# Two first-layer feature tiles in one product scheme, for thirteen more pairs of tiles: a tuned attention and feed-forward kernel on one Trainium2 core

## The chip, the core and the metric

The kernel runs on one core of one Trainium2 chip. A core has engines that each work through a list of instructions of their own, in the order of that list: TensorE does matrix products (PE in the profile, its weight loads PEld), VectorE element-wise work (DVE), ScalarE activations and copies (ACT), GpSimd (POOL) and SyncE (SP) here mostly start transfers. They meet through semaphores: an instruction that needs another engine's result waits, and everything behind it in its list waits with it. Products land in PSUM, which is divided into banks; all else is kept in SBUF. The metric is device microseconds of one execution, lower is better.

## The reference

All data is float32. The first half is a recurrence over 768 steps for 4 batches and 8 heads of 48 channels, and the second half a feed-forward layer over the 3072 tokens of 384 channels that it gives:

```python
for t in range(S):                                   # attention, per batch and head
    cur = np.einsum('bhd,bhe->bhde', u[None] * kt, vt)
    y[:, :, t] = np.einsum('bhd,bhde->bhe', rt, state + cur)
    state = wt[:, :, :, None] * state + np.einsum('bhd,bhe->bhde', kt, vt)

x = attn_out.transpose(0, 2, 1, 3).reshape(B * S, H * D)      # 3072 x 384
h = x @ w_in                                         # 384 -> 2048
g = h - np.tanh(h)
return (g @ w_out).astype(np.float32)                # 2048 -> 384
```

## The kernel before

The tokens are cut into 8 blocks of 384 (a batch and one of its halves each, numbered 0 to 7). The outer loop runs over the blocks, the inner over the 16 feature tiles f = 0 to 15 of 128 features. While a block goes through its feed-forward layer, the attention of the next block is threaded between its tiles, so that TensorE always has products to do. The order on every engine is the order in which the Python code issues the instructions. No scheduler changes it, and it was arranged by hand.

**A plain feature tile.** `first` (L887) multiplies three 128x128 pieces of `w_in` by the three 128x384 pieces of the block's tokens `xT`, which are summed in the PSUM bank `hp`. The profile counts two passes for each float32 product, so a tile has 6 passes of 384 columns. `slight` then has ScalarE read `hp` twice (two tanh, L975 and L976) and square the first (L979, with a second record for its accumulator), and VectorE multiplies the two (L894) to g. The first layer of the next plain tile needs `hp` free again, and so ScalarE's two reads of it done.

**The second layer in fewer products.** For two tiles, that is a pair q = f // 2, g @ w_out takes 15 products of 128x128 instead of 18 (`Fewer`). They work on sums of pieces of g, which VectorE makes (`form_g`, L998, two such sums of 128x128 in one instruction), and on sums of pieces of `w_out`, kept in `forms`. Of the five instructions with sums of g for a pair one stands at its first tile (`formed`), one at its second, and three (`held_back`, then `forming`) behind the next pair's first tile. Where that pair is joined, two of these three are put off once more, to its second tile (`carried`). The products of a pair come in two parts of six, one with the next pair's first tile and one with its second. The last three of the 15 ("others", numbers 12 to 14) are put off: those of pairs 0 to 3 come together at f = 9, twelve products into a bank of their own, which ScalarE then scales out to `o` (`self.half`, L1091).

**A joined pair.** `Twos` does the first layer of two feature tiles in one scheme: on the first two of the three contraction pieces and on two halves of the tokens (HB = 192 columns) it takes 7 products for what plainly takes 8; the third piece takes 4. So a joined pair has 11 products of 128x192 (L949, 22 passes of 192 columns) where two plain tiles have 6 of 128x384 (12 passes of 384). It needs five sums of pieces of `w_in` for the pair (`weight_forms`) and four sums of token pieces for the block (`token_forms`). The products land in both banks of a double scratch named `att_...` instead of `hp`. From there one ScalarE copy (L950) and four VectorE sums (L959) give h of both tiles in SBUF, and only then `slight` runs, on h in SBUF. A VectorE list around a joined pair reads: rest of the earlier work, the first of the four sums, the sum `formed` of the pair before, the other three sums. Then come sums of products (L1114), attention work, and what was carried.

**Which pairs are joined.** `JOINED` names them by block: pair 1 in blocks 3, 4 and 5, pairs 1 and 7 in block 6, and pairs 0 to 6 in block 7, 12 in all. Pair q covers the tiles f = 2q and 2q + 1. The sums of weights of pair 1 are made anew at f = 0 of each of the blocks 3 to 6 into the left-over end of a tile for v; the results lie in a borrowed attention tile, `ks`.

Around the places that the change touches, a stage of the profile is two tiles and what is threaded between. Pairs are written by block and number below, "pair 4 of block 3" for the tiles f = 8 and 9 of block 3.

## Time and profile before

| what | value | where it stands |
|---|---|---|
| median of 3 runs | 539.9 us (539.46 to 540.0) | times |
| time of the profiled execution | 539.97 us | times |
| its span on the core | 538.2 us | page, first line |
| TensorE clock granted | 0.998 of full | times |
| PE busy | 529.1 us, 98% of the span | page, part 1 |
| DVE busy | 442.8 us, 82% | page, part 1 |
| ACT busy | 307.1 us, 57% | page, part 1 |

The profiled execution took 1.8 us more than its span, and 0.1 us more than the median. The span runs from the first to the last record on the core. PE is busy in every one of the page's 40 slices at 90% or more except the first and the last. Since matmuls are pipelined, a record may begin while the one before ends, so durations of single passes add up to more than their stretch; what a pass costs in a row is the distance from its start to the next one's start. The same holds on DVE and ACT, where one instruction starts a little before the recorded end of the last.

### The profile page before, as it was taken

What the parts mean: (1) busy time and instruction counts of PE and PEld (TensorE: products, weight loads), DVE (VectorE), ACT (ScalarE), POOL (GpSimd) and SP (SyncE); (2) the same over time, 40 slices, a digit from 0 to 9 for tenths busy, and PEclk for the clock granted to TensorE, in tenths of its full rate; (3) what the DMA queues carried; (4) which work ended last, traced back from release to release, by engine and by line L of the source; (5) the groups of instructions that cost most, each with busy time, mean ns of one, the idle gap of its engine ahead of it and who ended that gap; (6) DMA issues with size and microseconds to landing.
All of it is one profiled execution on the core that took longest, in us unless ns stands there. A gap on an engine that the chain in (4) does not pass through costs nothing.

```text
span 538.2 us, 14868 instructions
## 1 busy us (share of the span) xinstructions
PE 529.1 (98%) x5820; PEld 419.5 (78%) x5820; DVE 442.8 (82%) x914; ACT 307.1 (57%) x707; POOL 9.2 (2%) x57
## 2 busy tenths in 40 slices
PE   7999999999999999999999999999999999999996
PEld 5756665678777777877878787787878877999994
DVE  7989997698879878887887969879689798867874
ACT  4899974665546564456446564375643654435450
POOL 1100000000000000000000000000000000000001
PEclk9999999999999999999999999999999999999999
DMA  7798732352311631163121642136232410100011
GB/s 277 242 393 337 246 124 71 109 128 67 118 38 60 163 118 57 47 146 120 63 57 45 150 118 66 51 79 174 62 98 58 98 55 16 43 1 2 10 35 48
DMA packets 53047, 56.34 MB, mean 105 GB/s; under 512 B 21488, under 2 KB 50928, under 8 KB 52976
## 3 DMA queue, kind: packets, MB, share of 16 engines
q1 hardware_dynamic: 52592, 55.18, 34.1%
q8 instruction: 49, 0.80, 0.6%
q14 instruction: 22, 0.18, 0.1%
q10 hardware_dynamic: 288, 0.10, 0.1%
q0 software_dynamic: 96, 0.07, 0.1%
HBM read 44.73 MB, written 4.72 MB: 92 GB/s over the span
## 4 chain that ended last, share of the span: by engine, by line
PE 96%; DVE 1%; DMA 0%; PEld 0%; issue 0%; ACT 0%; PEldq 0%; DVEq 0%; SPq 0%
PE hp L887 36%; PE acc L1079 27%; PE att L949 8%; PE att L1079 6%; PE acc L1030 6%; PE att L773 4%; PE att L496 2%; PE att L577 2%; PE acc L1057 1%; PE att L887 1%; PE acc L887 1%; PE hp L1079 0%; DMA states<-in_wT 0%; PE att L519 0%; DVE scores L504 0%
## 5 line engine op out<-in xcount | busy, mean ns | idle before, releaser
L887 PE MATMUL hp<-xT,w_sb 128*128 128x384 f32 x594 | 208.8, 488 | 0.0
L887 PEld LDWEIGHTS hp<-xT,w_sb 128*128 128x128 f32 x594 | 106.2, 190 | 56.6 <-ACT qa L976 0.3
L1079 PE MATMUL acc<-forms,g 128*128 128x128 f32 x972 | 136.0, 276 | 0.0
L975 ACT ACTIVATE h<-hp 128x384 f32<-128x384 f32 x99 | 48.9, 494 | 145.7 <-PE hp L887 145.7
L1079 PEld LDWEIGHTS acc<-forms,g 128*128 128x128 f32 x972 | 124.4, 192 | 7.7
L998 DVE TENSOR_TENSOR g<-g 128x256 f32<-128x256 f32 x270 | 106.5, 420 | 7.2 <-PE acc L1079 2.0
L894 DVE SCALAR_TENSOR_TENSOR g<-h,qa 128x384 f32<-128x384 f32 x112 | 62.1, 554 | 56.4 <-ACT h L979 55.4
L979 ACT ACTIVATE h<-h 128x384 f32<-128x384 f32 x113 | 59.1, 523 | 0.0
L1079 PE MATMUL acc<-w_sb,g 128*128 128x128 f32 x324 | 54.1, 276 | 0.0
L1079 PEld LDWEIGHTS acc<-w_sb,g 128*128 128x128 f32 x324 | 47.0, 192 | 7.6
L976 ACT ACTIVATE qa<-hp 128x384 f32<-128x384 f32 x99 | 48.5, 490 | 0.0
L1114 DVE TENSOR_TENSOR sums<-sums 128x256 f32<-128x256 f32 x84 | 33.1, 411 | 1.3 <-ACT sums L1091 0.9
L1030 PE MATMUL acc<-w_sb,sums 128*128 128x384 f32 x96 | 33.7, 487 | 0.0
L1079 PE MATMUL att<-w_sb,g 128*128 128x128 f32 x200 | 33.4, 275 | 0.0
L266 ACT ACTIVATE up<-raw 128x768 f16<-128x768 f32 (+1 forms) x32 | 32.8, 1095 | 0.0
L1079 PEld LDWEIGHTS att<-w_sb,g 128*128 128x128 f32 x200 | 29.0, 192 | 4.2
L1030 PEld LDWEIGHTS acc<-w_sb,sums 128*128 128x128 f32 x96 | 18.1, 190 | 12.3
L431 DVE TENSOR_TENSOR_SCAN post<-w,seed 128x780 f32<-128x780 f32 x14 | 24.9, 1777 | 0.9 <-DMA w<-in_wT 0.9
L419 DVE TENSOR_TENSOR_SCAN pre<-w,start 128x780 f32<-128x780 f32 x14 | 25.0, 1783 | 0.8
L949 PE MATMUL att<-xT,w_sb 128*128 128x192 f32 x120 | 25.4, 326 | 0.0
L979 ACT ACTIVATION_READ_ACCUMULATOR h<-h 128x1 f32 x113 | 22.7, 201 | 0.0
L949 PEld LDWEIGHTS att<-xT,w_sb 128*128 128x128 f32 x120 | 19.9, 190 | 0.0
(181 smaller groups left out, 654.2 us busy)
## 6 DMA issues: line engine op xcount, KB each, us to landing
raw<-in_weights SPq DMA_DIRECT2D x16, 768.0 KB, 7.6
w<-in_wT SPq DMA_DIRECT2D x7, 780.0 KB, 4.4
k<-in_kT SPq DMA_DIRECT2D x7, 768.0 KB, 5.2
r<-in_rT SPq DMA_DIRECT2D x7, 768.0 KB, 4.4
v_sb<-in_v SPq DMA_DIRECT2D x8, 576.0 KB, 4.9
k<-in_tokens SPq DMA_DIRECT2D x7, 576.0 KB, 4.0
r<-in_tokens SPq DMA_DIRECT2D x7, 576.0 KB, 5.3
out_y<-sums SPq DMA_DIRECT2D x18, 128.0 KB, 1.9
```

The costliest lines, as they stand in the source:

```text
L266: return lambda: nc.scalar.activation(out=to, in_=of, func=AF.Copy, scale=scale, bias=bias)
L419: return nc.vector.tensor_tensor_scan(out=self.tile("pre")[:, cols], data0=self.tile("w")[:, cols], data1=start[:, 0:n * NCH * LP], initia ...
L887: nc.tensor.matmul(hp, lhsT=w_in_sb[:, f, kc, :], rhs=xT[kc], start=(kc == KC - 1), stop=(kc == 0))
L894: return lambda: nc.vector.scalar_tensor_tensor(out=out, in0=in0, scalar=scalar, in1=in1, op0=op0, op1=ALU.mult)
L949: nc.tensor.matmul(to, lhsT=lhs, rhs=rhs, start=n == 0, stop=n + 1 == len(of))
L975: made = nc.scalar.activation(out=t, in_=h, func=AF.Tanh, scale=INNER / UPSCALE)
L976: nc.scalar.activation(out=by, in_=h, func=AF.Tanh, scale=OUTER / UPSCALE)
L979: nc.scalar.activation(out=t, in_=t, func=AF.Square, accum_out=top[:, n:n + 1])
L998: return lambda: nc.vector.tensor_tensor(out=G[:, to:to + 2], in0=two(G, g_at(q, a0), g_at(q, a1)), in1=two(G, g_at(q, b0), g_at(q, b1)), ...
L1030: nc.tensor.matmul(acc, lhsT=g[:, j * P:(j + 1) * P], rhs=w_out_sb[:, f, :], start=(f == self.first), stop=(f == NF - 1))
L1079: nc.tensor.matmul(to, lhsT=G[:, g_at(q, a), :], rhs=rhs, start=start, stop=stop, skip_group_check=True)
L1114: ops.append(lambda op=op, at=at: nc.vector.tensor_tensor(out=at[0], in0=at[1], in1=at[2], op=OPS[op]))
```

## The change

Thirteen more pairs are joined: pairs 3, 4 and 7 in the blocks 3, 4 and 5, pairs 3 and 4 in block 6 (pair 7 was joined there), and pairs 4 and 7 in block 2. In the blocks 2 to 6 all joined pairs now go through one object, `beside`.

- **Sums of weights** are made once and kept in a new SBUF tile, `kept`: those of pairs 3 and 4 in block 1 at f = 8 (five instructions, 128x256 each), of pair 7 in block 2 at f = 6 and of pair 1 in block 2 at f = 10 (five of 128x128 each). The five instructions at f = 0 of each of the blocks 3 to 6 go.
- **Sums of tokens** of a block lie in a new tile `turned`; they are made at f = 1, and now in block 2 too. Block 6 no longer makes its own at f = 13 for pair 7.
- **Results** h lie in a new tile `joint`, seven rows of 192 in place of eight.
- **The "others" of pairs 0 to 3**, at f = 9, go to the bank `hp` in every block with joined pairs after block 1, where they had a half of the double scratch.
- To make room, the scratch for POOL's dynamic transfers is set to 2048 bytes. A tag of a tile in a path that is taken only for other data changes from "s" to "h".

The order on ScalarE, in block 3 from the last tile of pair 3 on, before. Here `h<-hp` is the first tanh of a plain tile, `o<-att_123` the scaling out of the twelve others, and `ks<-...` copies of the next block's attention:

```order
L979 ACTIVATE h,top<-h 128x384
L554 COPY ks<-ks 128x2x2x128
L975 ACTIVATE h<-hp 128x384
L976 ACTIVATE qa<-hp 128x384
L979 ACTIVATE h,top<-h 128x384
L554 COPY ks<-ks 128x2x2x128
L975 ACTIVATE h<-hp 128x384
L976 ACTIVATE qa<-hp 128x384
L979 ACTIVATE h,top<-h 128x384
L1091 ACTIVATE o<-att_123 128x384
L554 COPY ks<-post 128x2x2x128 x3
L975 ACTIVATE h<-hp 128x384
```

and after the change:

```order
L957 COPY joint<-att_125 128x192
L982 ACTIVATE h<-joint 128x384
L983 ACTIVATE qa<-joint 128x384
L986 ACTIVATE h,top<-h 128x384
L559 COPY ks<-ks 128x2x2x128
L982 ACTIVATE h<-joint 128x384
L983 ACTIVATE qa<-joint 128x384
L986 ACTIVATE h,top<-h 128x384
L1098 ACTIVATE o<-hp 128x384
L559 COPY ks<-post 128x2x2x128 x3
L982 ACTIVATE h<-hp 128x384
```

Both tiles of pair 4 now read `joint`, which VectorE's sums fill, the scaling out stands behind the second of them as before, and its source is `hp`, the bank that the next tile's first layer (f = 10) writes.

The order on VectorE, in block 3 from the first tile of pair 3 (f = 6) to the second of pair 4 (f = 9), before. `k<-k,r` and `diagonal<-k` are two wide steps of the next block's attention:

```order
L894 SCALAR_TENSOR_TENSOR g<-h,qa 128x384
L1114 TENSOR_TENSOR sums<-sums 128x2x128
L998 TENSOR_TENSOR g<-g 128x256
L1114 TENSOR_TENSOR sums<-sums 128x2x128
L388 TENSOR_TENSOR k<-k,r 128x1152
L894 SCALAR_TENSOR_TENSOR g<-h,qa 128x384
L998 TENSOR_TENSOR g<-g 128x256 x4
L392 TENSOR_REDUCE diagonal<-k 128x3x4x2
L894 SCALAR_TENSOR_TENSOR g<-h,qa 128x384
L1114 TENSOR_TENSOR sums<-sums 128x2x128
L998 TENSOR_TENSOR g<-g 128x256
L1114 TENSOR_TENSOR sums<-sums 128x2x128
```

and after, from the first of pair 3's four sums on:

```order
L966 TENSOR_TENSOR joint<-joint,att_125 128x2x192
L1005 TENSOR_TENSOR g<-g 128x256
L966 TENSOR_TENSOR joint<-joint,att_126 128x384
L966 TENSOR_TENSOR joint<-joint,att_126 128x192
L966 TENSOR_TENSOR joint<-joint,att_126 128x384
L1121 TENSOR_TENSOR sums<-sums 128x2x128 x2
L393 TENSOR_TENSOR k<-k,r 128x1152
L1005 TENSOR_TENSOR g<-g 128x256
L899 SCALAR_TENSOR_TENSOR g<-h,qa 128x384
L1005 TENSOR_TENSOR g<-g 128x256
L397 TENSOR_REDUCE diagonal<-k 128x3x4x2
L899 SCALAR_TENSOR_TENSOR g<-h,qa 128x384
```

and then:

```order
L1005 TENSOR_TENSOR g<-g 128x256 x2
L966 TENSOR_TENSOR joint<-joint,att_125 128x2x192
L1005 TENSOR_TENSOR g<-g 128x256
L966 TENSOR_TENSOR joint<-joint,att_126 128x384
L966 TENSOR_TENSOR joint<-joint,att_126 128x192
L966 TENSOR_TENSOR joint<-joint,att_126 128x384
```

Eight sums of h came in. The sums of g of pair 2 that were carried, and the second tile's product of pair 3, now stand behind `k<-k,r` and `diagonal<-k`, and pair 4's sums of h behind all of these.

The order on TensorE, in block 3 from the end of the others to the first layer of f = 10, before:

```order
L1079 MATMUL att_123<-w_sb,g 128x128
L1079 MATMUL acc_600<-w_sb,g 128x128 x2
L1079 MATMUL acc_600<-forms,g 128x128 x2
L1079 MATMUL acc_599<-forms,g 128x128 x2
L887 MATMUL hp<-xT_1915,w_sb 128x384
```

and after:

```order
L1086 MATMUL hp<-w_sb,g 128x128
L1086 MATMUL acc_603<-w_sb,g 128x128 x2
L1086 MATMUL acc_603<-forms,g 128x128 x2
L1086 MATMUL acc_602<-forms,g 128x128 x2
L892 MATMUL hp<-xT_1923,w_sb 128x384
```

The list is the same but for the bank: the others now fill the `hp` that the last row needs empty, with six products of pair 3 between them.

The diff, cut to its core:

```diff
-JOINED = {3: (1,), 4: (1,), 5: (1,), 6: (1, NF // 2 - 1), 7: TWOS}
+BESIDE = (1, 3, 4, 7)
+JOINED = {2: (4, 7), 3: BESIDE, 4: BESIDE, 5: BESIDE, 6: BESIDE, 7: TWOS}
+FORMED = {(1, 8): (3, 4), (2, 6): (7, 7), (2, 10): (1, 1)}
...
+    kept = const.tile([P, 5 * len(BESIDE) * P], F32, name="kept", tag="kept")
+    turned = const.tile([P, 2 * NB], F32, name="turned", tag="turned")
+    joint = const.tile([P, 7 * HB], F32, name="joint", tag="joint")
...
-            nc.scalar.copy(out=h[:, 7], in_=e0[:, 1, 0:HB])
+            nc.scalar.copy(out=h[:, 3], in_=e0[:, 1, 0:HB])
...
-                by = beside if near else twos
+                by = beside if later else twos
...
-            if later and i in JOINED and f < 2:
-                if not f:
-                    beside, v_left, late_left = (Twos(1, 1), spare_tile("v_sb", NCP * DM), spare_tile("late", NB))
-                    for x in range(5):
-                        beside.form(x, v_left, x * P)
-                    beside.results(spare_tile("ks", NPAIR * NCP * P, work))
-                    spare += beside.weight_forms(0, 2, 1, 4, 3)
-                else:
-                    spare += beside.token_forms(here, beside.halves((v_left, 5 * P), (late_left, 0)))
+            if (i, f) in FORMED:
+                spare += beside.weight_forms(0, 2, 1, 4, 3, of=FORMED[i, f])
+            if later and i in JOINED and f == 1:
+                spare += beside.token_forms(here, beside.halves((turned, 0), (turned, NB)))
...
-                    spare = (twos.token_forms(here, twos.halves((post_left, left), (ks_left, left))) +
-                             twos.weight_forms(2, 3, 4) + spare)
+                    spare = twos.weight_forms(2, 3, 4) + spare
...
-                fewer.others(ps_a, range(4))
+                fewer.others(ps_a, range(4), hp if joined else None)
...
-    nc = bacc.Bacc("TRN2", target_bir_lowering=False, num_devices=1)
+    nc = bacc.Bacc("TRN2", target_bir_lowering=False, num_devices=1, dynamic_dma_scratch_size=2048)
```

More of the change, by code (lines that the diff above doesn't have):

```diff
@@ L823, in totals @@
             nxt = dense.tile([P, NB], F32, name="tot", bufs=3 if m < 8 else 2,
-                             tag={1: "h", 2: "s", 4: "qa"}.get(m, "o"))
+                             tag={1: "h", 2: "h", 4: "qa"}.get(m, "o"))
             nxt = nxt[:, 0:n * NB // (2 * m)]
@@ L900, with __init__ @@
     class Twos:
-        def __init__(self, base, n):
-            self.base, self.n = base, n
+        def __init__(self, pairs):
+            self.pairs = pairs
             self.forms, self.to = [None] * 5, []
         def form(self, x, t, at=0):
-            self.forms[x] = t[:, at:at + self.n * P].rearrange("p (j c) -> p j c", c=P)
+            n = len(self.pairs)
+            self.forms[x] = t[:, at:at + n * P].rearrange("p (j c) -> p j c", c=P)
         def halves(self, *tiles):
@@ L914, in results, with weight_forms @@
         def results(self, *tiles):
-            self.to = [t[:, 0:8 * HB].rearrange("p (n t) -> p n t", t=HB) for t in tiles]
-        def weight_forms(self, *which):
-            at = w_in_sb[:, 2 * self.base:2 * (self.base + self.n)]
-            at = at.rearrange("p (j two) k c -> p j two k c", two=2)
+            self.to = [t[:, 0:7 * HB].rearrange("p (n t) -> p n t", t=HB) for t in tiles]
+        def weight_forms(self, *which, of=None):
+            of = of or (self.pairs[0], self.pairs[-1])
+            at = w_in_sb[:, 2 * of[0]:2 * of[1] + 2].rearrange("p (j two) k c -> p j two k c", two=2)
             (a11, a12, a13), (a21, a22, a23) = ([at[:, :, i, k] for k in range(KC)] for i in range(2))
-            s1, s2, s3, s4, s5 = self.forms
+            x0, x1 = (self.pairs.index(j) for j in of)
+            s1, s2, s3, s4, s5 = (t if t is None else t[:, x0:x1 + 1] for t in self.forms)
             every = (("add", s1, a21, a22), ("sub", s2, s1, a11), ("sub", s3, a11, a21), ("sub", s4, a12, s2),
@@ L940, in begin @@
             (a11, a12, a13), (_, a22, a23) = ([w_in_sb[:, 2 * j + i, k] for k in range(KC)] for i in range(2))
-            s1, s2, s3, s4, s5 = (t[:, j - self.base] for t in self.forms)
+            s1, s2, s3, s4, s5 = (t[:, self.pairs.index(j)] for t in self.forms)
             t1, t2, t3, t4 = self.turned
@@ L959, in begin @@
             return [lambda of=of: nc.vector.tensor_tensor(out=of[0], in0=of[1], in1=of[2], op=ALU.add)
-                    for of in ((h[:, 0:5:4], twice(h[:, 7]), both(e0[:, 0, 0:NB])),
+                    for of in ((h[:, 0:5:4], twice(h[:, 3]), both(e0[:, 0, 0:NB])),
                                (h[:, 5:7], twice(h[:, 4]), both(e1[:, 0, 0:NB])),
@@ L1003, in any_h @@
         nc.scalar.activation(out=h, in_=of, func=AF.Copy, scale=1.0 / UPSCALE)
-        s, qa = (dense.tile([P, NB], F32, name=name, tag=name) for name in ("s", "qa"))
+        s, qa = (dense.tile([P, NB], F32, name=name, tag=name) for name in ("h", "qa"))
         th, qb, big = (inp.tile([P, 2 * HALF], F32, name=name, tag=tag)[:, 0:NB]
@@ L1304 @@
     acc += [ps_d.tile([P, BANK], F32, name=f"acc{j}", tag=f"acc{j}") for j in range(1, NB // P)]
+    beside = Twos(BESIDE)
+    for x in range(5):
+        beside.form(x, kept, x * len(BESIDE) * P)
+    beside.results(joint)
     rest, formed, extra, behind, due, summed = [], [], [], [], [], []
@@ L1375 @@
                 spare += [lambda n=n: form_w(n, 4 if f < 12 else 6, 2) for n in formed_w.get(f, ())]
-            if later and i in JOINED and f < 2:
-                if not f:
-                    beside, v_left, late_left = (Twos(1, 1), spare_tile("v_sb", NCP * DM), spare_tile("late", NB))
-                    for x in range(5):
-                        beside.form(x, v_left, x * P)
-                    beside.results(spare_tile("ks", NPAIR * NCP * P, work))
-                    spare += beside.weight_forms(0, 2, 1, 4, 3)
-                else:
-                    spare += beside.token_forms(here, beside.halves((v_left, 5 * P), (late_left, 0)))
+            if (i, f) in FORMED:
+                spare += beside.weight_forms(0, 2, 1, 4, 3, of=FORMED[i, f])
+            if later and i in JOINED and f == 1:
+                spare += beside.token_forms(here, beside.halves((turned, 0), (turned, NB)))
             if i == blocks_n - 2:
                 if f == 10:
-                    twos = Twos(0, NF // 2)
-                    left = twos.n * P
-                    k_left, r_left, post_left = (spare_tile(name) for name in ("k", "r", "post"))
-                    for x, t in enumerate((k_left, r_left, post_left)):
+                    twos = Twos(range(NF // 2))
+                    left = len(twos.pairs) * P
+                    k_left, r_left = (spare_tile(name) for name in ("k", "r"))
+                    for x, t in enumerate((k_left, r_left, spare_tile("post"))):
                         twos.form(x, t)
@@ L1393 @@
                 elif f == 13:
-                    ks_left = spare_tile("ks", NPAIR * NCP * P, work)
-                    twos.form(3, ks_left)
+                    twos.form(3, spare_tile("ks", NPAIR * NCP * P, work))
                     twos.form(4, spare_tile("v_sb", NCP * DM))
-                    spare = (twos.token_forms(here, twos.halves((post_left, left), (ks_left, left))) +
-                             twos.weight_forms(2, 3, 4) + spare)
+                    spare = twos.weight_forms(2, 3, 4) + spare
                     twos.results(*(spare_tile(name) for name in ("pre", "w")))
```

## The prediction

> **What bounds the kernel now.** I read the page's first part and its chain, then PE's waits, then the stages around joined and plain pairs in windows. The chain gives one row by engine, and PE's waits are five rows of which the first is the longest:

> ```profile
> span 538.2 us, 14868 instructions
> PE 529.1 (98%) x5820; PEld 419.5 (78%) x5820; DVE 442.8 (82%) x914; ACT 307.1 (57%) x707; POOL 9.2 (2%) x57
> PE 96%; DVE 1%; DMA 0%; PEld 0%; issue 0%; ACT 0%; PEldq 0%; DVEq 0%; SPq 0%
> PE att L314 <- POOL ident masks.py:199: 2.1, 1, 2.1
> ```

> PE is the chain: 96% of it, busy for 98% of the span. So a pass taken from PE is worth its length, as long as nobody else then comes last. The windows by engine show how near DVE is to that (a row is the stretch, its length, then busy time and count of PE, PEld, DVE, ACT and POOL; the last three numbers are granted clock, DMA share and GB/s). In order they are pair 1 of block 3 (joined), a joined pair of block 7, pair 3 of block 3 (plain), its pair 4 with the twelve others (plain), and f = 0 and 1 of block 4:

> ```profile
> 224.00:230.31 6.31, 6.31 (x48) 6.31 (x47) 4.43 (x8) 4.70 (x8) 0.00 (x0) 1.00 0.28 91
> 462.98:469.23 6.25, 6.25 (x48) 6.25 (x47) 4.43 (x11) 2.05 (x8) 0.00 (x0) 1.00 0.07 16
> 238.62:245.17 6.55, 6.55 (x39) 4.96 (x38) 6.45 (x13) 3.40 (x10) 0.00 (x0) 1.00 0.51 134
> 245.17:254.40 9.23, 9.23 (x63) 7.64 (x62) 7.91 (x16) 5.43 (x15) 0.00 (x0) 1.00 0.50 149
> 278.42:283.71 5.29, 5.29 (x39) 4.50 (x37) 4.77 (x12) 1.61 (x6) 0.00 (x0) 1.00 0.08 25
> ```

> PE has no gap in any of them. In the plain pair 3 DVE is busy for 6.45 of 6.55 us: that is where this change puts eight more sums of h. The same for DVE alone, tile 9 and the tile after it:

> ```profile
> 248.44:254.40 5.96, 4.64 (x11) 1.00 0.34 97
> 254.40:259.09 4.69, 1.15 (x4) 1.00 0.15 52
> ```

> In tile 9 DVE has 5.96 - 4.64 = 1.32 us of room, and 4.69 - 1.15 = 3.54 in tile 10. What is late catches up there.

> **What PE gains.** The eleven products of a joined pair in the chain, the first second-layer products behind them, and the weight loads' group on the page (busy, mean ns of one, idle before):

> ```profile
> 224.16 3.58 PE att L949 x22
> 227.57 1.05 PE L1079 MATMUL acc<-forms,g 128*128 128x128 f32 x8
> L949 PEld LDWEIGHTS att<-xT,w_sb 128*128 128x128 f32 x120 | 19.9, 190 | 0.0
> ```

> From 224.00 to 227.57 the 22 passes take 3.57 us, .162 each. The rest of a pair, products of the second layer, is the same in a joined and a plain pair. So a pair gains 6.55 - 6.25 = .30 to 6.55 - 6.31 = .24 by the windows; I take .295, which the block 7 row supports, where less is threaded in. Thirteen pairs give 3.84 us. If all else were hidden, that would be 539.97 - 3.84 = 536.1.

> [...]

> **What DVE and ACT pay in blocks 3 to 6.** Let S be PE's start of pair 3 (238.62 in block 3). These rows give DVE's prices; a price is the distance from a start to the next start. First the sums of h of a joined pair (the first, the sum of g after it, the other three, the next; the same three cut after the second), then a product, sums of products, k times r, a product, the diagonal's reduce, and a sum of g that must wait for its product:

> ```profile
> 225.85 0.56 DVE L959 TENSOR_TENSOR ks<-ks,att 128x384 f32<-128x384 f32 x1
> 226.32 0.42 DVE L998 TENSOR_TENSOR g<-g 128x256 f32<-128x256 f32 x1
> 227.78 1.41 DVE L959 TENSOR_TENSOR ks<-ks,att 128x384 f32<-128x384 f32 x3 [1.03 <-PE att L949]
> 229.10 0.42 DVE L998 TENSOR_TENSOR g<-g 128x256 f32<-128x256 f32 x1
> 227.78 0.94 DVE L959 TENSOR_TENSOR ks<-ks,att 128x384 f32<-128x384 f32 x2 [1.03 <-PE att L949]
> 240.10 0.56 DVE L894 SCALAR_TENSOR_TENSOR g<-h,qa 128x384 f32<-128x384 f32 x1
> 240.57 0.42 DVE L1114 TENSOR_TENSOR sums<-sums 128x256 f32<-128x256 f32 x1
> 240.91 0.42 DVE L998 TENSOR_TENSOR g<-g 128x256 f32<-128x256 f32 x1
> 241.58 1.36 DVE L388 TENSOR_TENSOR k<-k,r 128x1152 f32<-128x1152 f32 x1
> 242.85 0.56 DVE L894 SCALAR_TENSOR_TENSOR g<-h,qa 128x384 f32<-128x384 f32 x1
> 244.86 1.35 DVE L392 TENSOR_REDUCE diagonal<-k 128x24 f32<-128x1152 f32 x1
> 246.12 0.55 DVE L894 SCALAR_TENSOR_TENSOR g<-h,qa 128x384 f32<-128x384 f32 x1
> 252.31 0.54 DVE L894 SCALAR_TENSOR_TENSOR g<-h,qa 128x384 f32<-128x384 f32 x1
> 252.88 0.43 DVE L998 TENSOR_TENSOR g<-g 128x256 f32<-128x256 f32 x1
> ```

> So: first sum of h .47, the three 1.32, two of them .94; a sum of g or of products .34, to its end .42; k times r 1.27; reduce 1.26; product .47, or .57 where a sum of g needs it. In pair 1 the three begin 3.78 after PE's start, when the last product has landed, and DVE idles 1.03 before. In pair 3 likewise they begin at S + 3.78, since DVE is free of f = 5 by then. Then down the list of the order after: the three to 5.10; two sums of products, the second reading the first, .79 to 5.89 (estimate: .42 and .34, and a little for the wait); k times r to 7.16; sum of g to 7.50; product and sum of g .91 to 8.41; reduce to 9.67; product of pair 3's second tile to 10.14. Behind it stand two carried sums of g, the second reading the first: 10.14 to 10.56, and 10.67 to 11.09. Then pair 4: first sum at 11.01, .47 to 11.48; sum of g to 11.82; and two of the three, after which tile 8's h is whole, .94 to S + 12.76.

> PE meanwhile starts pair 4 at S + 6.26 and reaches its products 3.57 later, at 9.83; a product is two passes, .22 (8 passes in 1.05 above, .11 apart). The third reads the first carried sum and could start at 10.27: it waits till 10.61, .34. The fifth, then at 11.05, reads the second: .09. So .43 us in each of the blocks 3 to 6. It is nothing if DVE runs .43 ahead of my sum, and .85 if it runs .4 behind; I take the sum.

> Next ACT, whose rows are the first tanh of two joined tiles that follow each other, the scaling out of the others, and three copies behind it:

> ```profile
> 230.08 0.53 ACT L975 ACTIVATE h<-ks 128x384 f32<-128x384 f32 x1
> 231.42 0.52 ACT L975 ACTIVATE h<-ks 128x384 f32<-128x384 f32 x1
> 253.26 0.49 ACT L1091 ACTIVATE o<-att 128x384 f32<-128x384 f32 x1 [1.30 <-PE att L1079]
> 253.64 2.00 ACT L554 COPY ks<-post 128x512 uint16<-128x512 uint16 x3
> ```

> A tile costs 1.34 us. Tile 8's starts when h is whole, at 12.80, ends 14.14; a copy .62 (an estimate, 2.00 for three, less the overlap) to 14.76; tile 9's to 16.10; then the scaling out, .49, to S + 16.59, and PE sees `hp` free at 16.64. Before, that scaling out (253.26, S + 14.64) read a bank that nobody waited for; now f = 10's first layer does. Without a wait PE would be there at S + 15.78 (254.40) less .59 for two pairs, plus .43: 15.62. So it waits 1.02. Behind that first layer stand all of PE's later products, so nothing hides it. From f = 6 to f = 10 a block goes from 15.78 to 16.64: +.87. The bounds: -.59, if pair 4's sums come 1.5 us earlier, so that nobody waits; +1.3, if DVE runs .4 behind my sum, since that delays PE's second layer and the scaling out alike. DVE then has the 3.54 us of tile 10 to be on time again, and pair 7 starts clean.

> **Pair 7 (blocks 2 to 5), and the rest.** With S' PE's start of f = 14, these rows are the reciprocal, the scan, the product and the next step of block 3's end:

> ```profile
> 277.43 0.22 DVE L418 RECIPROCAL start<-whole 128x12 f32<-128x12 f32 x1
> 277.69 1.78 DVE L419 TENSOR_TENSOR_SCAN pre<-w,start 128x780 f32<-128x780 f32 x1
> 279.39 0.53 DVE L894 SCALAR_TENSOR_TENSOR g<-h,qa 128x384 f32<-128x384 f32 x1
> 279.84 0.95 DVE L445 TENSOR_TENSOR post<-k,post 128x768 f32<-128x768 f32 x1
> ```

> The sums of h end at S' + 5.10; four sums of products, one narrow, 1.45 (estimate, .42 each where the next reads it) to 6.55; sum of g to 6.89; product and sum .91 to 7.80; reciprocal .26, scan 1.70, product .45 to 10.21; two carried sums end at 10.63 and, as a product's sum stands between, at 11.31. PE starts f = 0 of the next block at S' + 6.26, and its six products end that stage's 5.29 us: they begin 3.96 in, the third at 10.66 (.02 late), the fifth at 11.12 (.24 late). So .26 is paid and .295 gained, -.03 a block, bounds -.295 (sums on time) and +.3. Block 6 had pair 7 joined already: 0.

> Block 2 gets pair 4 without pair 3. Its k times r and its stage before:

> ```profile
> 180.53 1.36 DVE L388 TENSOR_TENSOR k<-k,r 128x1152 f32<-128x1152 f32 x1
> 181.44:190.67 9.23, 9.23 (x63) 7.64 (x61) 8.54 (x17) 5.44 (x15) 0.00 (x0) 1.00 0.29 88
> ```

> k times r ends .4 us into the pair, when its products have not landed yet, so DVE is not behind: tile 8's h is whole 3.78 + .94 = 4.72 in, two tiles and a copy end 3.3 later, at 8.0, and the scaling out at 8.5; PE needs `hp` at 9.23 - .295 = 8.94. Hidden, -.295, with its pair 7 (-.03) -.33 in all. The new sums of weights are fifteen instructions of .34 (128x256) or less, 1.75 us in block 1 and 1.0 twice in block 2. I take 0, since they stand where DVE has room in the block shown (3.54 us in f = 10); if none of it were hidden they would cost 3.75, if a tenth .4. Five such go from f = 0 of each of the blocks 3 to 6, where DVE was busy for 4.77 of 5.29 us: 0 too, for DVE is not late there before, with -.3 at best where pair 7's sums would be late. The others in `hp` in block 7: `hp` lies idle there until f = 14, 0.

> Sum: -.33 + 3 x (.87 - .03) + .87 = +3.06, on 539.97 (.1 over the median): 543.0.

> **The rivals.** All hidden, 536.1: for it speak the 57% of ACT and the 82% of DVE; against it the 6.45 of 6.55 above. It decides at S + 15.1 for the end of the scaling out, 1.5 us before my sum. It is the one on the other side. Half hidden: the carried sums come in time, the bank's wait is left at about .65: a block then loses .65 - .59 = .06 in pairs 3 and 4 and gains .295 in pair 7, so .06 x 4 - 3 x .295 - .59 = -1.24, 538.7. The backlog lasts: DVE still late in f = 11 to 13, another .5 to 1 us in each of four blocks, 545 to 547; the 3.54 us idle speak against. The transfers: POOL's three, whose scratch gets small, stand in the first block (the second row is a transfer of the same chip with its time to landing):

> ```profile
> L793 POOL DMA_DIRECT2D xT<-late x3: 487/487/619, 17.6 to 18.6; - x3
> out_y<-sums SPq DMA_DIRECT2D x18, 128.0 KB, 1.9
> ```

> At two further landings of 1.9 us they would add up to 3.8 on the forecast, 546.8; they are issued within 1.0 us in the first 19 us, and I see no need of them then. Weight loads pace narrow passes: 22 x .190 = 4.18 us instead of 3.57 to 3.89, +.29 x 13 = +3.8, 543.7 alone; the 3.58 of the chain rules it out.

> **How the numbers follow.** My forecast .68 (its own range 541 to 545, from the bounds of the three waits taken halfway), all hidden .10, half hidden .12, lasting backlog .06, transfers .03, weight loads .01. Leaving out the first rival, and the top of the backlog, gives 538.5 to 545.2. 0.2% or 1.1 us is what a measurement of this kernel can tell from no change: faster is the first rival and most of the half hidden one, .17; same .06; slower .77.

> **What the profile after would show.** PE idle before the first layer of f = 10, waiting for ACT's `o<-hp`, about 1.0 us four times; PE waiting for a sum of g in four blocks, .34 and .09 a time, and at f = 0; joined pairs of 6.25 to 6.31 us where nothing waits; PE's busy time about 3.8 lower, near 525.3; DVE's about 23 higher by the thirteen pairs' sums. Wrong if the scaling out ends by S + 15.1, if DVE catches up inside pair 3, or if a joined pair takes longer beside attention work than in block 7.

## The result: 1.4% slower, by more than the waits that were forecast

The changed kernel took 547.21 us in the median of four runs (545.76 to 548.68), the kernel before 539.94 in the same session. The ratio is 1.0137 with an interval of 1.0101 to 1.0172. The forecast was 543.0 us, its range 538.5 to 545.2. The direction was right; the time lies above the range. Two of the four runs took 545.76 and 545.99, two, the profiled one among them, 548.43 and 548.68.

The profiled execution took 548.68 us, 8.7 us more than the one before (span 547.0 for 538.2). The page's first lines and chain, and PE's waits (in total, times, longest):

```profile
span 547.0 us, 14920 instructions
PE 531.2 (97%) x5950; PEld 439.2 (80%) x5950; DVE 464.8 (85%) x961; ACT 310.4 (57%) x720; POOL 9.2 (2%) x57
PE 86%; DVE 7%; ACT 3%; issue 1%; DMA 1%; PEld 0%; SPq 0%; PEldq 0%; DVEq 0%
```

```profile
PE hp L892 <- ACT o L1098: 2.9, 4, 0.7
PE att L778 <- issue: 2.5, 2, 1.9
PE att L316 <- POOL ident masks.py:199: 2.1, 1, 2.1
PE att L501 <- issue: 1.5, 1, 1.5
PE att L501 <- ACT k L461: 1.0, 1, 1.0
PE acc L1086 <- DVE g L1005: 0.8, 4, 0.2
```

The chain is no longer PE's alone. Two rows were forecast, `hp` waiting for the scaling out (four times) and `acc` waiting for sums of g (four times). Two more were not: "issue", time in which PE waited for nothing that the profile shows. The stages by engine (stretch, length, busy time of PE, PEld, DVE, ACT, POOL, clock, DMA share, GB/s): pair 4 of block 2; pairs 3 and 4 of block 3; f = 0 of block 4; then f = 12 and f = 13 of block 6, and the end of that f = 13.

```profile
181.72:190.65 8.93, 8.93 (x72) 8.93 (x71) 6.86 (x15) 5.39 (x15) 0.00 (x0) 1.00 0.31 92
239.51:245.77 6.26, 6.26 (x49) 6.26 (x47) 5.25 (x11) 2.06 (x8) 0.00 (x0) 1.00 0.88 255
245.77:256.14 10.37, 9.44 (x73) 9.05 (x71) 10.13 (x21) 6.56 (x18) 0.00 (x0) 1.00 0.26 80
279.98:285.64 5.66, 5.66 (x38) 4.63 (x37) 5.59 (x12) 2.65 (x8) 0.00 (x0) 1.00 0.35 104
458.36:466.71 8.35, 6.41 (x212) 5.20 (x211) 8.00 (x20) 1.61 (x6) 0.18 (x2) 1.00 0.24 73
466.71:471.74 5.03, 5.03 (x20) 3.88 (x19) 2.18 (x3) 3.00 (x8) 0.00 (x0) 0.66 0.11 28
468.00:471.74 3.74, 3.74 (x16) 3.02 (x14) 0.89 (x2) 1.82 (x6) 0.00 (x0) 0.54 0.14 33
```

The first four are the forecast's stages: pair 4 of block 2 gains (9.23 before), pair 3 gains (6.55), pair 4 of block 3 loses (9.23), f = 0 loses (5.29). The fifth and sixth are new. Before, they were

```profile
453.40:459.60 6.20, 6.20 (x212) 5.21 (x211) 5.73 (x17) 1.61 (x6) 0.18 (x2) 1.00 0.32 97
459.60:462.98 3.38, 3.38 (x26) 2.58 (x19) 3.35 (x5) 2.77 (x7) 0.00 (x0) 1.00 0.10 21
```

so block 6 loses 2.15 us in f = 12, where PE stands still, and 1.65 in f = 13, where PE is busy throughout but at a granted clock of 0.54 over its last 3.74 us (the trace's clock records have 0.50 for 3.41 us from 468.10 on). The rows of PE where it stood still, in blocks 2 and 6:

```profile
204.17 1.55 PE L778 MATMUL att<-scores,v_sb 64*48 64x64 f32 x93 [0.53 <-issue]
...
466.57 0.21 PE L778 MATMUL att<-scores,v_sb 64*48 64x64 f32 x1 [1.94 <-issue]
```

Where the 8.7 us are, by the distance between the starts of the blocks' first matmuls: block 2 +0.24, blocks 3, 4 and 5 +1.03 to +1.05 each, block 6 +5.13, block 7 -0.05; before block 1 +0.27. Of these, 0.82 (block 2, f = 12) and 3.80 (block 6, f = 12 and 13) are the new part, 4.6 us. The rest of blocks 2 to 7 is 3.8 us, which the prediction put at 3.06.

### The profile page after: what moved, and what is told of

Its sections match the earlier page's. It is cut to its first block, busy times and chain, and to the rows that moved or that the text cites. A ratio compares the mean times of both kernels' runs of the same rounds, so it can differ in the third digit from the quotient of the medians.

```text
span 547.0 us, 14920 instructions
## 1 busy us (share of the span) xinstructions
PE 531.2 (97%) x5950; PEld 439.2 (80%) x5950; DVE 464.8 (85%) x961; ACT 310.4 (57%) x720; POOL 9.2 (2%) x57
## 3 DMA queue, kind: packets, MB, share of 16 engines
HBM read 44.73 MB, written 4.72 MB: 90 GB/s over the span
## 4 chain that ended last, share of the span: by engine, by line
PE 86%; DVE 7%; ACT 3%; issue 1%; DMA 1%; PEld 0%; SPq 0%; PEldq 0%; DVEq 0%
PE hp L892 26%; PE acc L1086 23%; PE att L956 14%; PE acc L1037 6%; PE att L778 4%; PE att L1086 3%; PE att L501 2%; DVE joint L966 2%; PE att L582 2%; PE hp L1086 1%; PE acc L1064 1%; DVE g L1005 1%; PE att L892 1%; DMA r<-in_rT 1%; DVE k L393 1%
## 5 line engine op out<-in xcount | busy, mean ns | idle before, releaser
L892 PE MATMUL hp<-xT,w_sb 128*128 128x384 f32 x438 | 155.2, 491 | 2.9 <-ACT o L1098 2.9
L1086 PE MATMUL acc<-forms,g 128*128 128x128 f32 x972 | 138.3, 278 | 0.8 <-DVE g L1005 0.8
L892 PEld LDWEIGHTS hp<-xT,w_sb 128*128 128x128 f32 x438 | 78.7, 191 | 48.6 <-ACT o L1098 3.7
L982 ACT ACTIVATE h<-hp 128x384 f32<-128x384 f32 x73 | 36.0, 493 | 102.0 <-PE hp L892 101.9
L1086 PE MATMUL acc<-w_sb,g 128*128 128x128 f32 x324 | 55.3, 280 | 0.0
L956 PE MATMUL att<-xT,w_sb 128*128 128x192 f32 x250 | 53.0, 326 | 0.0
L966 DVE TENSOR_TENSOR joint<-joint,att 128x384 f32<-128x384 f32 (+1 forms) x72 | 34.6, 501 | 17.6 <-PE att L956 10.0
L982 ACT ACTIVATE h<-joint 128x384 f32<-128x384 f32 x36 | 18.7, 519 | 44.6 <-DVE joint L966 44.6
L956 PEld LDWEIGHTS att<-xT,w_sb 128*128 128x128 f32 x250 | 41.5, 190 | 0.0
L983 ACT ACTIVATE qa<-hp 128x384 f32<-128x384 f32 x73 | 35.7, 489 | 0.0
## 6 DMA issues: line engine op xcount, KB each, us to landing
out_y<-sums SPq DMA_DIRECT2D x18, 128.0 KB, 1.9
```

Source lines behind the costliest of these rows:

```text
L892: nc.tensor.matmul(hp, lhsT=w_in_sb[:, f, kc, :], rhs=xT[kc], start=(kc == KC - 1), stop=(kc == 0))
L956: nc.tensor.matmul(to, lhsT=lhs, rhs=rhs, start=n == 0, stop=n + 1 == len(of))
L966: return [lambda of=of: nc.vector.tensor_tensor(out=of[0], in0=of[1], in1=of[2], op=ALU.add) for of in ((h[:, 0:5:4], twice(h[:, 3]), both ...
L982: made = nc.scalar.activation(out=t, in_=h, func=AF.Tanh, scale=INNER / UPSCALE)
L983: nc.scalar.activation(out=by, in_=h, func=AF.Tanh, scale=OUTER / UPSCALE)
L1086: nc.tensor.matmul(to, lhsT=G[:, g_at(q, a), :], rhs=rhs, start=start, stop=stop, skip_group_check=True)
```

## What stood at f = 12: pieces of PE's program

At f = 12 TensorE runs 192 small passes of attention (L778), 384 instructions with their weight loads, in 2.8 us. The page's third part has a queue of the kind "instruction", `q8 instruction: 49, 0.80, 0.6%`, 49 packets of 16 KB each. They keep step with PE: it has 12,424 records before and 12,486 after, loads and NO_OPs included, 254 and 255 for a packet, so they are taken here for the pieces of its program. After the change packet k, counted from 0, begins as PE is at its record 256 k + 151 to 410 (median 222). The starts of two of these packets, worked out from the trace's packet records, beside the start of f = 12:

```
                      block 2: f=12   piece     block 6: f=12   piece    f=12 of blocks 2, 6 takes
before                  198.63       197.29       453.40       458.82        6.21   6.20
after                   198.62       201.94       458.36       464.13        7.03   8.35
```

In block 6 the piece comes 5.4 us after the start of f = 12 before, and 5.8 after the change. What differs is where PE stands then. A joined pair has 44 instructions for PE (11 products, each two loads and two passes), two plain tiles 24 and their NO_OPs, 36 or 42. So the burst of block 6 stands 62 instructions later in the program, and its end at the place where PE waited for 1.94 us, till 1.56 us after the end of the packet that began inside the burst. In block 2 the burst moved by 2 instructions only, but the packet began 4.65 us later, as the load of `r` (199.03 to 202.02 us) ended.

The place of the wait is the same each time. Counted in PE's records, weight loads included, all nine waits for "issue" at an f = 12 in the kept traces stand at number 193 (once 192) of a stretch of 256 (after the change at records 5057 and 11457, that is 19 x 256 + 193 behind packet 18 and 44 x 256 + 193 behind packet 43), and PE goes on 1.3 to 1.6 us after the end of the packet that had come last. After the change block 6's burst comes to that place twice, the second time with its last pass; before, it ended 62 records short of the second. The seven "issue" waits of 1.0 to 1.7 us in the boot (the work ahead of the first feed-forward layer) stand at number 193 too.

Two theories went into the experiments: *code* (PE's fetch, set off by the moved program), with the waits of the prediction beside it, and rivals that put the 4.6 us on transfers, the small scratch or chance.

## The experiments

**e1: the changed kernel with the program's phase of before.**

```diff
+NOPS = {(2, 10): (3, 2, 2), (3, 0): 0, (3, 1): 0, (3, 4): 0, (3, 5): 0, (4, 0): 1, (5, 0): 0, (5, 1): 0, (5, 4): 0, (5, 5): 0, (6, 0): 1}
...
-            for _ in range(apart):
+            for _ in range(apart if isinstance(apart, int) else apart[kc]):
...
-                h = first(here, f, to[:, 0:NB], SPACED[i][f > 12 + (i < 2)])
+                h = first(here, f, to[:, 0:NB], NOPS.get((i, f), SPACED[i][f > 12 + (i < 2)]))
```

> The changed kernel, with NO_OPs behind matmuls of plain tiles taken out (62 in all, in blocks 2 to 6), so that the number of TensorE instructions ahead of each block's f = 12 is again what it was before the change. Theory 'code': in block 6, f = 12, PE ran through a burst of 384 small instructions into a piece of its program that had not been fetched yet (1.94 us of idle time, then a granted clock of 0.54 that makes f = 13 1.65 us longer), because the joined pairs moved where the program's 16 KB pieces begin. It expects no such idle time in block 6, so 3.6 us less than the profiled run of the changed kernel (548.7), and perhaps the 0.5 us of block 2 as well: 544.2 to 545.1. Rival 'transfers': the late fetch comes from the transfers' timing or the small scratch, and the phase has nothing to do with it: 545.8 to 548.7 as before, with the idle time still there.

It took 545.08 us (ratio 1.0086, 1.0063 to 1.0109). f = 12 of block 2, then f = 12 and 13 of block 6:

```profile
199.48:206.50 7.02, 6.51 (x213) 5.37 (x211) 6.81 (x14) 1.61 (x6) 0.18 (x2) 1.00 0.40 117
459.17:465.37 6.20, 6.20 (x212) 5.21 (x211) 5.86 (x18) 1.61 (x6) 0.18 (x2) 1.00 0.22 64
465.37:468.75 3.38, 3.38 (x26) 2.58 (x19) 3.38 (x5) 2.77 (x7) 0.00 (x0) 1.00 0.27 74
```

Block 6 is what it was before the change: 62 NO_OPs fewer took the 3.80 us away, the fall of the clock with them. Block 2's wait stayed, so the moved program is not what brought it. The median fell by 2.1 us, less than 3.8, since the 3.80 are those of the profiled run alone.

**e2: the kernel before with the changed kernel's phase in block 6** (as e1's edit, with two NO_OPs more per matmul, at f = 11 up to four, in the plain tiles f = 0 to 11 of block 6, 62 in all).

> The kernel before, with 62 more NO_OPs behind matmuls in block 6, f = 0 to 11, so that its f = 12 burst stands where the changed kernel has it among the program's pieces. Theory 'code': PE idles at the end of that burst for 1.3 to 2 us for nothing that the profile shows, and the clock falls after it as in the changed kernel: 541.2 to 543.6. Rival 'transfers': 539.9, within 0.5, and no idle time there.

541.96 us (1.0034, 1.0018 to 1.005), and PE's wait in the burst:

```profile
462.45 0.21 PE L774 MATMUL att<-scores,v_sb 64*48 64x64 f32 x1 [1.59 <-issue]
```

Instructions that do nothing brought the wait into a kernel that had not had it, at the same last pass of the burst. With e1 this settles *code* for block 6. The clock did not fall after these 1.59 us.

**e3: the scaling out ahead of the second tile's activations**, on e1.

```diff
-            if fewer and f == 9:
+            if fewer and f == 9 - joined:
```

> As e1, and the twelve others with their scaling out are issued one tile earlier in the code where the pair is joined: PE's and DVE's lists stay as they are, and on ACT the scaling out of hp moves ahead of the second tile of pair 4, behind its first. Theory 'bank' (the prediction's term): f = 10 waits only because the scaling out stands behind the second tile's activations, so the wait of four blocks goes: the stretch f = 8 and 9 falls from 10.37 us to 9.3 to 9.5 (what is left is PE waiting for the carried sums of g), 3.4 to 4.2 us less than e1. Rival 'DVE': DVE is what is late, and the wait comes back elsewhere (f = 10 or 11): less than 2 us below e1.

543.33 us (1.0071, 1.0054 to 1.0087), 1.75 less than e1. Pair 4 of block 3 and f = 10:

```profile
245.37:254.85 9.48, 9.29 (x73) 9.09 (x72) 9.26 (x18) 5.32 (x14) 0.00 (x0) 1.00 0.25 86
254.85:259.88 5.03, 5.03 (x116) 3.75 (x115) 4.03 (x10) 5.03 (x13) 0.14 (x2) 1.00 0.00 0
```

The wait for `hp` is gone as *bank* had it: 0.89 us less in f = 8 and 9, in each of four blocks. But f = 10 took 5.03 us for 4.80, ACT being busy all through (in block 2, where nothing had waited, 5.04 for 4.69), and a wait of 0.54 for code appeared at f = 12 of block 3. So neither theory's whole sum came out: the mechanism was the forecast's, and about a quarter of the gain was given back one tile later.

**e4: only the small scratch**, on the kernel before (`dynamic_dma_scratch_size=2048`).

> The kernel before with only the scratch for POOL's dynamic transfers set to 2048 bytes. The theories 'code' and 'bank' expect no change: 539.5 to 540.3. Rival: the small scratch slows the first block's transfers, which would show as the 0.3 to 0.5 us by which the changed kernel starts its feed-forward later: 540.3 to 541.5.

540.31 us (1.0008, 0.9995 to 1.002): no difference. What varied was the boot: PE's first layer began at 23.3 to 25.1 us in the profiled runs of this case, whatever the kernel, with or without "issue" waits of 0.2 to 1.7 us at L501's line. In e1, e2, e9 and e10 the granted clock also fell to 0.50 for 3.41 us at 22 to 23 us, and their block 1 began at 88.9 to 89.4 us; without that fall it began at 87.2 to 88.1. So medians of a few runs can differ by a microsecond for that alone, and the stretches by block say more.

**e5: sums of weights of pair 1 at f = 14 instead of f = 10 of block 2**, on e1 (`(2, 14): (1, 1)` in `FORMED`).

> e1 (the phases of before), and the sums of weights of pair 1 formed at f = 14 of block 2 instead of f = 10. In e1 the wait for code at block 2's f = 12 was still there (7.02 us for 6.21), with the same number of instructions ahead. Theory 'run-ahead': DVE's 1.0 us more at f = 10 leaves DVE with no idle time there, so PE's sequencer, which waits for DVE's results, runs less far ahead and asks for its next piece of code only when the load of r is on the way; the piece came at 202.7 and before at 197.3. It expects the piece at about 197 to 198 and f = 12 at 6.2 us, 0.8 less in all. Rival 'chance': the order of the fetch and the load varies from run to run or goes by the instruction count, and f = 12 stays near 7.0.

544.64 us (1.0081, 1.0062 to 1.01). f = 12 of block 2, and f = 0 of block 3 behind it:

```profile
197.89:204.09 6.20, 6.20 (x213) 5.21 (x211) 6.06 (x12) 1.60 (x6) 0.18 (x2) 1.00 0.43 129
213.72:220.40 6.68, 5.77 (x39) 4.64 (x37) 6.61 (x17) 2.65 (x8) 0.00 (x0) 1.00 0.29 88
```

The piece came at 196.56, ahead of the load, and the wait went. The sums, now behind pair 7's, made f = 0 1.0 us longer instead.

**e6: pair 4 alone**, with e5's place for the sums and the phases of before.

```diff
+BESIDE = (1, 4, 7)
+JOINED = {2: (4,), 3: (1, 4), 4: (1, 4), 5: (1, 4), 6: BESIDE, 7: TWOS}
+FORMED = {(1, 8): (4, 4), (2, 6): (7, 7), (2, 14): (1, 1)}
```

> The changed kernel with only pair 4 added in blocks 2 to 6 (and pair 1 and block 6's pair 7 as before), NO_OPs so that the phases are those of before, sums of weights of pair 1 at f = 14. Theory 'bank': as in block 2 of the changed kernel DVE is not behind when pair 4 comes alone, the scaling out ends before f = 10 needs hp, and f = 8 and 9 take 8.94 us instead of 9.23 in five blocks: 1.5 us less than before, 538.5. Rival 'DVE': in blocks 3 to 6 k times r comes later than in block 2, so pair 4 alone already waits, 0.3 to 1 us a block: 539.9 to 542.

538.64 us, faster than the kernel before (0.9962, 0.9948 to 0.9976). That is 1.6 us, of which blocks 2 to 6 of the profiled run show 0.58; where the rest lies is not shown. f = 12 of block 2, and pair 4 and f = 10 of block 3:

```profile
198.47:205.54 7.07, 6.50 (x212) 5.36 (x210) 6.83 (x14) 1.60 (x6) 0.18 (x2) 1.00 0.39 116
245.87:254.80 8.93, 8.93 (x72) 8.93 (x71) 7.45 (x16) 5.38 (x15) 0.00 (x0) 1.00 0.56 179
254.80:259.50 4.70, 4.70 (x116) 3.57 (x115) 3.42 (x9) 4.02 (x10) 0.14 (x2) 1.00 0.02 3
```

Pair 4 is free where it stands alone: 8.93 us with no wait, f = 10 unchanged. So pair 4 costs something only behind a joined pair 3. Block 2's wait for code is back, with the same work on DVE around f = 10 as in e5; its piece came at 201.85. That takes *run-ahead* away as a full reason.

**e7: pair 3 alone in blocks 3 to 6** (`BESIDE = (1, 3, 7)`, and so on; block 2 has no joined pair).

> The changed kernel with only pair 3 added in blocks 3 to 6 (pair 4 plain, the others of f = 9 in the double scratch as before), the phases of before. By the prediction's chain DVE ends the carried sums of g at 10.56 and 11.09 us after pair 3's start, and a plain f = 8 brings PE to the third product that needs them at 6.26 + 1.94 + 0.44 = 8.64: it waits 1.9 us, so f = 8 takes 5.0 to 5.4 us instead of 3.27 and the kernel 4 x (1.9 - 0.3) = 6 us more: 545 to 547. Rival: the sums are not what PE waits for, pair 3 alone is hidden, 538.7.

551.35 us (1.0208, 1.0188 to 1.0228), more than either side had. PE's wait for sums of g (0.8 in all in the changed kernel), then f = 8 of block 3, and the first part of f = 9 of block 4:

```profile
PE acc L1087 <- DVE g L1006: 7.3, 4, 1.8
244.73:250.32 5.59, 3.76 (x20) 2.63 (x19) 5.52 (x11) 4.42 (x11) 0.00 (x0) 1.00 0.00 0
316.01:319.70 3.69, 3.69 (x9) 2.02 (x8) 3.59 (x10) 0.00 (x0) 0.00 (x0) 0.54 0.00 0
```

The wait of 1.8 us is the one that the prediction's chain gives for a plain f = 8; with it f = 8 took 2.3 us longer (5.59 for 3.28), and a block 2.03. So it is pair 3 that DVE cannot take. Alone it costs twice what pairs 3 and 4 cost together (0.95 a block), since by that chain a plain f = 8 brings PE to the late sums sooner. In blocks 4 and 6 the clock then fell to 0.50 for 3.41 us (0.54 and 0.55 over 3.7) and f = 9 took 7.65 us for 5.96, which no theory had expected. Both put the time above the 545 to 547 that were expected.

**e8: all sums of g ahead of the attention work at a joined pair's second tile**, on e3.

```diff
-                ops, carried = forming[:1] + rest + formed + spare, forming[1:]
+                ops = forming[:1] + rest + formed + forming[1:] + spare
```

> e3, and at the second tile of a joined pair DVE makes all of the earlier pair's sums of g ahead of the attention work (the diagonal's reduce in pair 3, the reciprocal and the scan in pair 7) instead of carrying two of them behind it. Theory 'carried sums': f = 8 and 9 fall from 9.48 to 8.94 in four blocks, f = 0 from 5.67 to 5.29 in blocks 3 to 6; 4 x 0.92 = 3.7 less than e3's 543.3: 539.6, and less where the late code fetches of f = 12 go as well. Rival 'scan': the scan and the reduce come 0.9 us later and PE waits for the attention's work instead: no better than e3.

541.51 us (1.0023, 1.0009 to 1.0037). In order f = 0, pair 1, pair 4 and f = 10 of block 3:

```profile
215.66:220.94 5.28, 5.28 (x38) 4.49 (x37) 5.11 (x11) 2.65 (x8) 0.00 (x0) 1.00 0.37 112
224.89:231.49 6.60, 6.58 (x48) 6.28 (x47) 5.95 (x13) 4.70 (x8) 0.00 (x0) 1.00 0.62 151
246.05:254.99 8.94, 8.94 (x73) 8.94 (x71) 8.73 (x18) 5.13 (x14) 0.00 (x0) 1.00 0.29 90
254.99:260.10 5.11, 5.09 (x117) 3.76 (x116) 4.75 (x12) 5.11 (x13) 0.14 (x2) 1.00 0.00 0
```

Both waits for carried sums are gone, as *carried sums* had it: 8.94 and 5.28. But pair 1 takes 6.60 us and f = 10 5.11, in e3 6.31 and 5.03, so 0.37 of the 0.92 us a block came back, and two waits for code stood in blocks 2 and 4. The time fell by 1.8 us, half of what the theory had; the rival's "no better than e3" did not come true either.

**e9 and e10: 28 NO_OPs more ahead of block 2's burst**, on e1 and on e6.

> e1, with 28 TensorE instructions more ahead of block 2's f = 12 (NO_OPs behind plain tiles f = 0 to 4 of block 2), so that PE enters the program piece that ends in the burst 28 instructions earlier and asks for the next while the load of k, not that of r, is on the way. Theory 'behind the load': the piece comes between the two loads, at 196 to 198 us, instead of 202.7, and f = 12 of block 2 takes 6.2 us, 0.8 less than in e1; the other blocks' bursts stay clear of a piece's end: 544.3. Rival: it is not the order of fetch and load; f = 12 of block 2 stays near 7.0 and the time at 545.1.

> e6 (pair 4 alone in blocks 2 to 6) with the same 28 instructions more. Theory 'behind the load': the 0.8 us that e6 still lost at f = 12 of block 2 go as well, f = 8 and 9 take 8.94 us in five blocks: 537.8 to 538.2, faster than the kernel before by 0.4%. Rival: as e6, 538.6.

e9 took 544.69 us (1.0071, 1.0051 to 1.009), e10 539.25 (0.9979, 0.9967 to 0.9992). f = 12 of block 2 in e9, the same 6.36 as in e10:

```profile
199.79:206.15 6.36, 6.36 (x212) 5.32 (x210) 6.15 (x12) 1.60 (x6) 0.18 (x2) 1.00 0.42 129
```

All but 0.16 us of the wait went, but not as expected: the piece came at 202.24 and 202.36, not between the two loads but in the middle of that of `r` (200.2 to 204.3 in e9). In e9 that is 2.45 us after the start of f = 12, in e1 3.21. e10's blocks 2 to 6 are together 1.3 us shorter than before (1.5 expected), its boot in the profiled run 1.5 us longer; its median of 539.25 does not stand apart from e6's.

**e11: pair 2 as well, on e10** (`BESIDE = (1, 2, 4, 7)`). This kernel leaves out eight instructions that mask scores (L510; 11 of them for the 19 in e10, where one takes 0.97 us of DVE on the mean), so its time is rather too short.

> e10, and pair 2 (f = 4 and 5) joined too in blocks 3 to 6. DVE was idle for 1.50 us in f = 4 and 0.1 in f = 5 of these blocks, and four sums of h cost 1.8 us. Theory 'room' (a pair can be joined where DVE's idle time ahead of the next need covers its sums): they nearly fit, PE's next need is the carried sums of pair 1 at f = 6, which come ahead of the attention work there, 4 x 0.3 = 1.2 us less than e10: 536.8. Rival 'carried sums': f = 6 is plain, so PE reaches the third product 2.4 us after its start, and waits for sums carried past f = 5's work, 0.3 to 1.8 us a block as in e7: 538 to 544.

539.95 us (0.9995, 0.9981 to 1.0009): no gain even so. Pair 2 of block 3 takes 8.46 us (229.54 to 238.00) where the two plain tiles took 8.31:

```profile
PE att L502 <- DVE joint L967: 0.9, 4, 0.2
```

PE's scores need the double scratch that the sums of h are still reading, a wait that neither theory had. Blocks 3 to 6 are 0.15 us longer each than in e10.

## Why the prediction was wrong, and where it was right

**The gain of a pair** (0.295) was right: 8.93 for 9.23, 6.25 to 6.26 for 6.55, and the same gain stands wherever nothing waits (pair 4 in e6 and e8). PE's busy time did not fall by 3.8 to 525.3 as forecast, but rose from 529.1 to 531.2: in f = 0 of block 4 all 5.66 us count as busy (5.29 before), two late passes being recorded with 377 ns for 275, and the time at the lower clock counts too (1.65 us more).

**The chain of blocks 3 to 6** was right to a few hundredths. With S = 239.51 in block 3, ACT and DVE of the changed kernel:

```profile
251.34 1.40 DVE L966 TENSOR_TENSOR joint<-joint,att 128x384 f32<-128x384 f32 x3
252.30 0.52 ACT L982 ACTIVATE h<-joint 128x384 f32<-128x384 f32 x1 [3.81 <-DVE joint L966]
255.62 0.47 ACT L1098 ACTIVATE o<-hp 128x384 f32<-128x384 f32 x1
256.14 1.24 PE L892 MATMUL hp<-xT,w_sb 128*128 128x384 f32 x3 [0.73 <-ACT o L1098]
```

Tile 8's activations begin at S + 12.79 (forecast 12.80), the scaling out at 16.11 (16.10), PE's f = 10 at 16.63 (16.64; less the 15.78 of before that is 0.86, where the sum has 0.87). The profile's own rows put less on the waits, 0.73 and 0.19, than the stage lost. e3 removed the bank's part, e8 the carried sums'. The sum missed 0.1 a block in f = 10 (4.80 for 4.70), where it had DVE on time again; ACT, whose three copies there end at 257.99, 1.85 us after PE's start (before 1.2), may be why, but no run shows it. The sums of weights, put at nothing, cost nothing: block 1 takes 63.00 us before and after, f = 10 of block 2 4.69.

**Pair 7** was a little too good: f = 0 takes 5.66 for 5.29, 0.37 where 0.26 stood, so +0.08 instead of -0.03 a block. Those two terms, 0.1 and 0.11 over four blocks, make up the 3.8 for 3.06 to within 0.1.

**The step that failed** is the sum itself: "Sum: -.33 + 3 x (.87 - .03) + .87 = +3.06" holds only waits between engines and takes PE's program for present. It counted the passes that joining removes, not the instructions that it adds and the NO_OPs that go with plain tiles, though these move the program's pieces under the burst of f = 12. That cost 3.80 us in block 6 of the profiled run (e1 takes it away, e2 brings the wait into the kernel before). A late piece of program also cost 0.82 in block 2, where the moved program is not the reason. With block 6's part taken away, e1's 545.08 lies just inside the range. No rival held a late piece of program. The rivals themselves: all hidden and half hidden did not occur; the lasting backlog was 0.1 us, not 0.5 to 1, a block; the small scratch for POOL's transfers did nothing (e4); weight loads did not pace the joined pairs, which took 6.25 to 6.31 us.

**What stays open.** What decides whether block 2's piece gets ahead of the load of `r`: e5 and e7 had it ahead (196.6, 197.2), as the kernel before; the changed kernel, e1, e3, e6 and e8 had it as that load ended (201.4 to 202.7), e9, e10 and e11 inside it (200.2 to 202.4), and neither DVE's lateness nor the phase sorts them. That the load held it up is argued from these times, not shown. And what makes the clock fall in one run and not in another. The changed kernel's runs of 545.76 and 545.99 us had a granted clock of 0.999 and 0.998 on the mean, the other two 0.997. By estimate 3.41 us at half speed alone bring it to 0.997 (1 - 3.41 x 0.5 / 547), so those two did not have the fall. That is 1.65 of the 2.6 us; the rest is not shown.

## What to carry to other kernels

Where a wait ends last is worth a list walked down in order, start to next start: pair 4 alone costs nothing (e6), pair 3 alone 2.03 us a block (e7), and for both together the chain met the start of f = 10 to 0.02 us. PE, busy for 98% of the span before, stood still for 1.94 us at the end of a burst that 62 instructions more had moved, and did not there with 62 NO_OPs fewer (e1): count the instructions that a change adds ahead of each burst of short ones, and if the same work waits for "issue" afterwards, move NO_OPs before looking for another cause. Of a wait taken away at one place, 0.2 to 0.4 us a block came back at others (e3, e8), most plainly in f = 10 of e3, where ACT had no idle time left.
